# A fixed emitted order for attention pieces and MLP groups in a fused attention and MLP kernel

## The chip, the core and the metric

The kernel runs on one core of a Trainium2 chip. The time is device microseconds (us) of that core, as a median of several executions. The profile's span runs from the first to the last instruction and is a few us shorter. PE is the TensorE matmul engine, DVE is VectorE, ACT is ScalarE, POOL is GpSimd and SP is SyncE.

## The reference

Eight batches of eight heads, 576 tokens and 64 columns of q, k and v go through linear attention. Its output, 4608 tokens of 512 columns, goes through a two-layer MLP with squared ReLU.

```python
q_p = phi(q, cos_w, sin_w)     # relu(x)*cos beside relu(x)*sin: 128 features
k_p = phi(k, cos_w, sin_w)
kv  = einsum('bhsf,bhsd->bhfd', k_p, v);  z = sum(k_p, axis=2)
num = einsum('bhsf,bhfd->bhsd', q_p, kv)
den = einsum('bhsf,bhf->bhs', q_p, z)[..., None] + 1e-06
x   = (num / den)              # rearranged to [4608, 512]
h   = x @ w_in                 # 512 -> 2048: "the first matmul"
out = relu(h)**2 @ w_out       # 2048 -> 512: "the second matmul"
```

## The kernel before

A batch of attention has three sorts of work on PE. `kz` is 40 matmuls of 65 columns. Then each of the five slices of tokens takes eight transposes (`tps`), eight matmuls (`numh`) and four more transposes. Between them DVE copies a result out of PSUM or divides. The tail of each batch has 64 tokens, the other slices 128.

```python
def attention_batch(b):
    ...                                            # loads, K features, V cast on ACT, kz
    for j, rows in slices:
        ...                                        # qp: cosine half on DVE, sine half on ACT
        for h in range(H):                         # PE
            nc.tensor.transpose(tps[:, h, :rows], qp[:rows, h, :], ident[:rows, :rows])
        nc.vector.tensor_copy(out=qpT[:, :, :rows], in_=tps[:, :, :rows])     # DVE
        for half in range(2):
            ...                                    # numh matmuls on PE; den, rden, attn on DVE
        for blk in range(NB):                      # PE
            nc.tensor.transpose(tps2[:, blk, :rows], attn[...], ident[:rows, :rows])
        nc.vector.tensor_copy(out=xT_dest(b, j, rows), in_=tps2[:, 0:NB, :rows])

def mlp_chunk(c):                                  # 512 tokens: 64 + 64 matmuls of 512 columns
    for hb in range(HB): ...                       # hps (PE), relu (ACT), square (DVE)
    for tt in range(NTT): ...                      # yps (PE), copy (ACT), store (SP)

for b in range(B):
    attention_batch(b)
for c in range(NCH):
    mlp_chunk(c)
```

The source puts all attention first. The instructions don't run in that order: a scheduler orders each engine's instructions, and it moves MLP matmuls up among the attention.

## Time and profile before

| | |
|---|---|
| median of three executions | 393.36 us (392.95 to 394.4) |
| span of the profiled execution | 388.8 us |
| PE busy | 335.3 us, 86% |
| pure MLP at the end | 13.81 us per 64 matmuls, 216 ns each |
| all 1152 MLP matmuls at that rate | 248.6 us |

These are lines of the page for the kernel before: busy tenths in 40 slices of 9.7 us each, where 9 is 90% or more, then the granted PE clock in tenths.

```profile
PE   0014586999999797999999999999999999999995
PEclk9999999899899698999999999999999999999999
```

PE does almost nothing in the first three slices of the span and is mostly full from the eighth on. The last part of the chain of waits, in order of time (start us, length us, what), is MLP alone.

```profile
204.81 13.81 PE yps L298 x64
218.62 13.81 PE hps L283 x64
...
356.75 13.81 PE hps L283 x64
370.57 13.83 PE yps L298 x64
```

That leaves 388.8 - 248.6 = 140 us which are not MLP at full rate: the start, and what attention costs after its gaps are filled with MLP. The three largest waits of PE in this kernel (who waited for whom: us in total, times, longest) are these.

```profile
PE kz L203 <- ACT kp L175: 22.5, 1, 22.5
PE tps L268 <- DVE attn L260: 9.4, 10, 1.1
PE numh L244 <- DVE qpT L235: 5.7, 9, 1.1
```

The first is the start. The other two are rare: 10 and 9 times, where attention has 40 slices of tokens (eight batches of five). The rest was covered by MLP matmuls. The clock's behaviour can be read from PE's timeline before (start us, length us, line, operation, count).

```profile
66.55 0.28 PE L268 MATMUL tps<-ident,attn 128*128 128x128 bf16 x2 [1.04 <-DVE attn L260]
...
67.58 3.11 PE L283 MATMUL hps<-xT,w1sb 128*128 128x512 bf16 x7
...
70.79 1.46 PE L283 MATMUL hps<-xT,w1sb 128*128 128x512 bf16 x6
```

After a thin stretch (one in which PE has little to do) seven matmuls take 3.11 us, 427 ns from start to start; soon after, six of the same shape take 1.46 us. The rate had halved against the 216 ns of pure MLP, then came back.

### The profile page before, as it was taken

Reading aid. Unit: us, or ns where it says so; the run is one execution under the profiler, and the core shown is the slowest. Engines: PE = TensorE matmul, PEld = TensorE weight load, DVE = VectorE, ACT = ScalarE, POOL = GpSimd, SP = SyncE. Lnnn points to the kernel's source line nnn. Section 1 sums busy time; section 2 is a strip of 40 time slices with the busy share of each in tenths; the row PEclk is TensorE's granted clock in tenths of the full one; section 3 lists DMA queues with packets and bytes.
Section 4 is the critical chain, followed back from the end, with each engine's and each line's share of the span. In section 5 each row is a group of like instructions: output and inputs, shape, how many; then the busy total and the mean of one; then the engine's idle time right before and its main releaser. Section 6 shows DMA issues by size and latency. Waiting matters only on the chain.

```text
span 388.8 us, 5849 instructions
## 1 busy us (share of the span) xinstructions
PE 335.3 (86%) x2272; PEld 173.0 (44%) x2272; DVE 173.0 (44%) x553; ACT 185.3 (48%) x319; POOL 2.9 (1%) x10
## 2 busy tenths in 40 slices
PE   0014586999999797999999999999999999999995
PEld 0013444565555454655544444444444444444442
DVE  1002757879687888584870150240330420420410
ACT  1063718689565758323642461551551642633621
POOL 3000000000000000000000000000000000000000
PEclk9999999899899698999999999999999999999999
DMA  8999861958859424242001101202102103002013
GB/s 218 225 214 304 258 200 25 362 198 253 248 166 306 131 78 139 65 127 66 1 2 52 57 0 54 56 0 64 46 0 83 27 6 77 28 27 79 4 27 83
DMA packets 45755, 42.32 MB, mean 109 GB/s; under 512 B 13984, under 2 KB 40608, under 8 KB 45728
## 3 DMA queue, kind: packets, MB, share of 16 engines
q1 hardware_dynamic: 43136, 37.76, 32.7%
q0 software_dynamic: 2592, 4.19, 5.8%
q8 instruction: 18, 0.29, 0.3%
q14 instruction: 9, 0.07, 0.1%
HBM read 36.70 MB, written 9.44 MB: 119 GB/s over the span
## 4 chain that ended last, share of the span: by engine, by line
PE 79%; DVE 8%; DMA 6%; SPq 2%; issue 2%; ACT 1%; ACTq 0%
PE yps L298 32%; PE hps L283 31%; DMA Qb<-in_q_dram 6%; PE tps L231 5%; PE kz L203 4%; PE tps L268 3%; PE numh L244 3%; DVE qpT L235 2%; SPq L156 2%; DVE attn L260 1%; DVE kp L167 1%; DVE qp L215 1%; DVE xT L273 1%; DVE den L252 1%; ACT vext L181 1%
## 5 line engine op out<-in xcount | busy, mean ns | idle before, releaser
L283 PE MATMUL hps<-xT,w1sb 128*128 128x512 bf16 x576 | 138.2, 389 | 0.5 <-DVE xT L273 0.5
L298 PE MATMUL yps<-w2sb,gT 128*128 128x512 bf16 x576 | 132.7, 382 | 1.6 <-DVE gT L292 0.8
L292 DVE TENSOR_TENSOR gT<-rt 128x512 bf16<-128x512 bf16 x144 | 60.4, 420 | 129.3 <-ACT rt L291 128.3
L291 ACT ACTIVATE rt<-hps 128x512 bf16<-128x512 f32 x144 | 85.3, 596 | 46.9 <-PE hps L283 45.0
L298 PEld LDWEIGHTS <-gT 128*128 128x128 bf16 x576 | 55.2, 98 | 63.8 <-issue 1.8
L283 PEld LDWEIGHTS <-w1sb 128*128 128x128 bf16 x576 | 55.3, 100 | 61.9 <-issue 4.6
L306 ACT COPY ysb<-yps 128x512 f32<-128x512 f32 x36 | 21.0, 585 | 84.0 <-PE yps L298 83.8
L203 PE MATMUL kz<-vext,kp 128*128 128x65 bf16 (+1 forms) x320 | 26.4, 204 | 27.7 <-ACT kp L175 22.5
L223 ACT ACTIVATE qp<-Qb,sin_col 128x512 bf16<-128x512 f32 x32 | 22.9, 719 | 27.8 <-PE tps L231 13.3
L203 PEld LDWEIGHTS <-kp 128*128 128x128 bf16 (+1 forms) x320 | 18.5, 100 | 34.6 <-ACT kp L175 24.6
L231 PE MATMUL tps<-ident,qp 128*128 128x128 bf16 (+1 forms) x320 | 29.3, 236 | 4.1 <-ACT qp L223 4.1
L260 DVE TENSOR_TENSOR attn<-numh,rden 128x256 bf16<-128x256 f32 (+1 forms) x80 | 32.1, 414 | 0.2
L268 PE MATMUL tps<-ident,attn 128*128 128x128 bf16 (+1 forms) x160 | 23.2, 232 | 9.6 <-DVE attn L260 9.4
L235 DVE COPY qpT<-tps 128x1024 bf16<-128x1024 bf16 (+1 forms) x40 | 25.3, 634 | 11.8 <-PE tps L231 11.3
L181 ACT CAST vext<-Vb 128x512 bf16<-128x512 f32 x32 | 18.4, 611 | 18.6 <-DMA Vb<-in_v_dram 18.6
L231 PEld LDWEIGHTS <-qp 128*128 128x128 bf16 (+1 forms) x320 | 21.9, 109 | 5.8 <-ACT qp L223 4.2
L268 PEld LDWEIGHTS <-attn 128*128 128x128 bf16 (+1 forms) x160 | 12.5, 103 | 25.8 <-DVE attn L260 17.6
L244 PE MATMUL numh<-kvz,qpT 128*128 128x65 bf16 (+1 forms) x320 | 18.7, 204 | 5.7 <-DVE qpT L235 5.7
L244 PEld LDWEIGHTS <-qpT 128*128 128x128 bf16 (+1 forms) x320 | 14.8, 107 | 19.0 <-DVE qpT L235 15.3
L175 ACT ACTIVATE kp<-Kb,sin_col 128x512 bf16<-128x512 f32 x32 | 21.7, 713 | 0.5 <-DMA Kb<-in_k_dram 0.5
L273 DVE COPY xT<-tps 128x512 bf16<-128x512 bf16 (+1 forms) x40 | 15.8, 394 | 11.5 <-PE tps L268 11.3
L215 DVE TENSOR_SCALAR qp<-Qb,cos_col 128x512 bf16<-128x512 f32 x32 | 15.1, 476 | 10.4 <-DMA Qb<-in_q_dram 10.4
(24 smaller groups left out, 74.0 us busy)
## 6 DMA issues: line engine op xcount, KB each, us to landing
Kb<-in_k_dram SPq DMA_DIRECT2D x8, 1024.0 KB, 7.8
Vb<-in_v_dram SPq DMA_DIRECT2D x8, 1024.0 KB, 10.8
Qb<-in_q_dram SPq DMA_DIRECT2D x8, 1024.0 KB, 5.5
out_dram<-ysb SPq DMA_DIRECT2D x40, 128.0 KB, 2.3
out_dram<-ysb SPq DMA_DIRECT2D x16, 256.0 KB, 2.4
w1sb<-in_moe_w_in_dram POOLq DMA_DIRECT2D x1, 2048.0 KB, 17.9
w2sb<-in_moe_w_out_dram POOLq DMA_DIRECT2D x1, 2048.0 KB, 32.2
Kt<-in_k_dram SPq DMA_DIRECT2D x8, 128.0 KB, 8.9
```

Source lines behind the costliest of these rows:

```text
L181: nc.scalar.copy(out=vext[:rows, j, :, 0:D], in_=vsrc)
L203: nc.tensor.matmul(out=kz[:, hh, :], lhsT=kp[:rows, j, h, :], rhs=vext[:rows, j, h, :], start=(ji == 0), stop=(ji == len(slices) - 1),)
L223: nc.scalar.activation(out=qp[:rows, :, D:F], in_=qsrc, func=ACTF.Relu, scale=sin_col[:rows, j : j + 1],)
L231: nc.tensor.transpose(tps[:, h, :rows], qp[:rows, h, :], ident[:rows, :rows])
L235: nc.vector.tensor_copy(out=qpT[:, :, :rows], in_=tps[:, :, :rows])
L244: nc.tensor.matmul(out=numh[:rows, hh, :], lhsT=qpT[:, h, :rows], rhs=kvz[:, h, :], start=True, stop=True,)
L260: nc.vector.tensor_tensor(out=attn[:rows, half * HH : half * HH + HH, :], in0=numh[:rows, :, 0:D], in1=rden[:rows].unsqueeze(2).to_broadca ...
L268: nc.tensor.transpose(tps2[:, blk, :rows], attn[:rows, 2 * blk : 2 * blk + 2, :], ident[:rows, :rows],)
L283: nc.tensor.matmul(out=hps[:, :], lhsT=w1sb[:, kb, hb * P : (hb + 1) * P], rhs=xT[:, kb, t0 : t0 + CH], start=(kb == 0), stop=(kb == KB - 1),)
L291: nc.scalar.activation(out=rt[:, :], in_=hps[:, :], func=ACTF.Relu)
L292: nc.vector.tensor_tensor(out=gT[:, hb, :], in0=rt[:, :], in1=rt[:, :], op=ALU.mult)
L298: nc.tensor.matmul(out=yps[:, :], lhsT=gT[:, hb, tt * P : (tt + 1) * P], rhs=w2sb[:, hb, :], start=(hb == 0), stop=(hb == HB - 1),)
```

## The change

The change has three intents. The order of every engine is fixed as emitted. The attention of batches 2 to 7 is put in pieces between groups of MLP matmuls, and the first matmul runs ahead of the second, so that the second matmul never waits for the square. All transposes stay on PE. Evictions also become wider (1024 columns for the first matmul), the V cast moves from ACT to POOL, and weights and later batches load behind the first two batches. The core of the diff, with cuts:

```diff
+PE_TRANSPOSE_BATCHES = 8
 ...
+    def att_v(b, j):
+        nc.gpsimd.tensor_copy(out=vexts[b % 2][:rows, j, :, 0:D], in_=piece("v", b, j))
 ...
+    def att_q(b, j):
+        qp = att.tile([P, H, F], BF16, name="qp", tag="qp", bufs=3)
+        feats(qp, piece("q", b, j), j, rows)                  # DVE and ACT
 ...
+        if b < PE_TRANSPOSE_BATCHES:
+            tq = ps_h.tile([P, H, P], BF16, name="tq", tag="hps", bufs=2)
+            for h in range(H):
+                nc.tensor.transpose(tq[:, h, :rows], qp[:rows, h, :], ident[:rows, :rows])
+            nc.vector.tensor_copy(out=qpT[:, :, :rows], in_=tq[:, :, :rows])
 ...                                                       # else: transposes by DMA
+    def att_out(b, j):          # num on PE; den, rden, x on DVE; tx on PE; copies to xT on DVE
 ...
-    for b in range(B):
-        attention_batch(b)
-    for c in range(NCH):
-        mlp_chunk(c)
+    with tc.manual_schedule():
+        ...
+        for b in range(2):                                    # the opening: no MLP in it
+            ...
+            att_kv(b, 0)
+            att_kv(b, 1)
+            for j in range(NS):
+                att_q(b, j)
+                att_out(b, j)
+        ...
+        gemm1_with_k(0, B)
+        gemm1_with_k(1, B)
+        for r in range(NCH):                                  # a round; b = r + 2
+            ...
+            for tt in range(NTT):
+                gemm2(r, tt)                                  # 16 matmuls
+                if b < B:
+                    if tt == 0:
+                        att_kv(b, 0)
+                        att_kv(b, 1)
+                        for j in range(NS):
+                            att_q(b, j)
+                    elif tt == 1:
+                        att_out(b, 0)
+                        att_out(b, 1)
+                        att_out(b, 2)
+                    elif tt == 2:
+                        att_out(b, 3)
+                        att_out(b, 4)
+            if r + 2 < NCH:
+                gemm1_with_k(r + 2, b + 1)
```

## The prediction

> **What bounds it now.** PE. The page gives PE 335 of 388.8 us (86%). From 204.8 us on, the chain of waits is pure MLP, 64 matmuls per 13.81 us (216 ns each), so all 1152 MLP matmuls need 248.6 us. The other 140 us are: no real PE work until about 29 us (loads, V casts), then eight attention batches. Between 29 and 204.8 us, 320 MLP matmuls (69 us) ran as filler in the attention's gaps, so attention costs about 13 us a batch beyond the MLP, of which 8.8 us is PE work (timeline: kz 40 x 73 ns, numh 8 in 0.55-0.6, transposes 8 in 0.45 and 4 in 0.25).
>
> **What the change does.** Little work is removed (fewer, wider evictions; V casts go from ACT to POOL). The order becomes literal on every engine. PE takes no filler, so each PE-DVE-PE round trip inside a piece is PE idle time.
>
> *Opening.* Batches 0 and 1 run alone, with no MLP. Loads no longer share with the weights; loads without them show 340-386 GB/s, so V0 is in at about 9 us, POOL casts end at about 12 (estimate; the Trainium skill, GPSIMD Engine Reference, Engine selection, calls one-input work roughly line-rate; no trace here shows it yet), kz ends at 16. Each slice is then serial: 8 cold transposes 0.87, copy 0.69, numh 0.62, den 0.16, reciprocal 0.17, multiply about 0.68 (estimated from 256 columns at 0.415), transposes 0.43, copy 0.42, next features 0.48, plus hops: 4.95 us. Ten slices and the second kz: first MLP matmul at about 73 us.
>
> *Rounds with attention (6).* kz 2.8. Queries: kz end, ACT eviction 0.38, ACT sine feature 0.72 before the first transpose; then per slice transposes 0.46, DVE copy 0.69, DVE feature of the next slice 0.48 and hops, 1.73: section 8.7 with 2.3 us of PE work. Outputs: numh 0.55, den+reciprocal+multiply 1.0, transposes 0.25, hops: 1.96 per slice, 9.8 with 4 us of PE work. Sum 21.3 us a round, 12 of it PE idle.
>
> *Clock.* The Trainium skill (TensorE: Matmul & The Clock Gate, Part 1) states half clock after an idle window of about 3.4 us and recovery after as long a busy one. The trace before agrees: after the sparse 62-67 us, seven hps matmuls take 3.11 us (427 ns, not 216), then full speed. Each sparse section should make the following group of 16 MLP matmuls about 1.5 us longer and its own transposes slower: about 4.5 us a round.
>
> ACT in the first matmul's groups: eviction of 1024 about 1.02 plus sine feature 0.72 equals PE's 1.73 per pair: about 0.5 us a round.
>
> **Sum.** Opening 73; two first chunks 29; six rounds of 27.6+21.3+4.5+0.5 = 323; last rounds 55; tail 4; launch difference 4.6 (393.4 against 388.8): 489. I lean a little lower for overlap I miss: **482 us, 445 to 515**. Chances: faster 0.03, same 0.03, slower 0.94.
>
> **What would show it.** First hps matmul at 65-80 us. In rounds: tq waits for DVE qp and the copy, tx waits for the DVE multiply, each several tens of us of PE idle in the groups; PE busy share falls to about 65-75%; granted clock below 0.95; first matmul's groups nearly gapless; windows of pure MLP at the end still 13.81 us per 64.
>
> **What would make it wrong.** Opening much shorter than 73 (warm clock, quicker slices); clock staying full in rounds (27 us less); DVE and PE pieces overlapping more than the literal order allows; POOL casts or POOL-issued loads arriving late (longer).

## The result, and the profile after

The changed kernel took 499.62 us (498.64 to 500.66, 4 runs) against 393.17 us for the kernel before. The ratio is 1.2708 (95% interval 1.2678 to 1.2738). Here and below, a ratio is the mean time of one kernel's runs over that of the kernel before in the same rounds, so it is not quite the ratio of the medians quoted. Executions over 1.5% slower than the fastest of the same kernel are left out of the means.

The same lines of the page, now for the changed kernel in slices of 12.4 us:

```profile
PE   0545439995689666985689567986689567999996
PEclk9999999995799768995899677995899778999999
```

PE is idle in the first slice of the span, about half busy in the next five, full for three, and then shows six rounds in which its busy share and its clock fall and rise together. These are its main waits for other engines.

```profile
PE tx L242 <- DVE x L225: 49.8, 40, 1.4
PE tq L197 <- DVE qp L145: 36.1, 30, 1.3
PE tq L197 <- ACT qp L153: 11.2, 10, 1.3
```

The counts are the point. There are 40 slices of tokens, and PE waited before `tx` 40 times and before `tq` 40 times. Before the change, the corresponding waits were 10 for `attn` and one for `qp`. The Trainium skill says that PE keeps matmuls in program order and only pulls weight loads ahead (TensorE: Matmul & The Clock Gate, Part 2). The trace agrees: in the rounds, ready MLP matmuls stand behind the 60 waits before `tq` and `tx` and don't overtake them.

One slice of the opening (start us, length us, engine, what) shows the serial chain.

```profile
23.64 1.01 PE L197 MATMUL tq<-ident,qp 128*128 128x128 bf16 x8 [1.13 <-DVE qp L145]
24.69 0.69 DVE L198 COPY qpT<-tq 128x1024 bf16<-128x1024 bf16 x1 [1.20 <-PE tq L197]
25.44 0.62 PE L210 MATMUL num<-kvz,qpT 128*128 128x65 bf16 x8 [0.79 <-DVE qpT L198]
26.54 0.69 DVE L225 TENSOR_TENSOR x<-num,rden 128x512 bf16<-128x512 f32 x1
27.28 0.61 PE L242 MATMUL tx<-ident,x 128*128 128x128 bf16 x4 [1.22 <-DVE x L225]
28.90 1.01 PE L197 MATMUL tq<-ident,qp 128*128 128x128 bf16 x8 [1.00 <-DVE qp L145]
```

A bracket is the idle time of the line's own engine just before it, and what ended it. From one `tq` to the next is 5.26 us, in which PE works for 2.2. The first MLP matmul starts at 74.84 us. One round, from PE's timeline:

```profile
160.99 3.62 PE L298 MATMUL yps<-w2sb,gT 128*128 128x512 bf16 x16
164.45 1.50 PE L176 MATMUL kz<-vext,kp 128*128 128x65 bf16 x20
166.41 1.50 PE L176 MATMUL kz<-vext,kp 128*128 128x65 bf16 x20 [0.46 <-ACT kvz L183]
168.99 1.03 PE L197 MATMUL tq<-ident,qp 128*128 128x128 bf16 x8 [1.09 <-ACT qp L153]
171.30 1.01 PE L197 MATMUL tq<-ident,qp 128*128 128x128 bf16 x8 [1.27 <-DVE qp L145]
...
178.64 5.59 PE L298 MATMUL yps<-w2sb,gT 128*128 128x512 bf16 x16
184.07 0.42 PE L210 MATMUL num<-kvz,qpT 128*128 128x65 bf16 x8
185.71 0.40 PE L242 MATMUL tx<-ident,x 128*128 128x128 bf16 x4 [1.22 <-DVE x L225]
...
190.02 5.04 PE L298 MATMUL yps<-w2sb,gT 128*128 128x512 bf16 x16
...
198.73 3.63 PE L298 MATMUL yps<-w2sb,gT 128*128 128x512 bf16 x16
202.20 13.98 PE L268 MATMUL hps<-xT,w1sb 128*128 128x512 bf16 x64
```

Taken by the starts, the four groups of `yps` took 3.46, 5.43, 4.88 and 3.47 us for the same 16 matmuls. The middle two follow thin stretches of 14.2 and 5.9 us, and were slow in all six rounds. The fourth also follows a thin stretch, of 3.8 us, but was slow in only one round of the six (5.15 us). The whole time after splits up at the starts of groups as follows.

| part | predicted us | measured us |
|---|---|---|
| to the first MLP matmul | 73 | 74.8 |
| two chunks of the first matmul | 29 | 30.3 |
| six rounds with attention | 323 | 332.8 (55.5 on average) |
| last rounds without attention | 55 | 55.3 |
| tail, and launch outside the span | 8.6 | 6.4 |

### The profile page after: what moved, and what is told of

It reads as the page before. It is cut to its first block, busy times and chain, and to the rows that moved or that the text cites. A ratio compares the mean times of both kernels' runs of the same rounds, so it can differ in the third digit from the quotient of the medians.

```text
span 497.9 us, 5606 instructions
## 1 busy us (share of the span) xinstructions
PE 371.0 (75%) x2272; PEld 190.5 (38%) x2272; DVE 164.4 (33%) x359; ACT 152.6 (31%) x207; POOL 57.9 (12%) x92
## 5 line engine op out<-in xcount | busy, mean ns | idle before, releaser
L298 PE MATMUL yps<-w2sb,gT 128*128 128x512 bf16 x576 | 152.1, 428 | 0.0
L276 ACT ACTIVATE rt<-hps 128x1024 bf16<-128x1024 f32 x72 | 73.7, 1023 | 59.6 <-PE hps L268 57.2
L277 DVE TENSOR_TENSOR gT<-rt 128x1024 bf16<-128x1024 bf16 x72 | 49.9, 693 | 114.4 <-ACT rt L276 114.4
L197 PE MATMUL tq<-ident,qp 128*128 128x128 bf16 (+1 forms) x320 | 36.1, 286 | 47.3 <-DVE qp L145 36.1
L242 PE MATMUL tx<-ident,x 128*128 128x128 bf16 (+1 forms) x160 | 17.7, 244 | 49.8 <-DVE x L225 49.8
L198 DVE COPY qpT<-tq 128x1024 bf16<-128x1024 bf16 (+1 forms) x40 | 25.5, 638 | 84.5 <-PE tq L197 84.5
L197 PEld LDWEIGHTS <-qp 128*128 128x128 bf16 (+1 forms) x320 | 27.5, 131 | 55.6 <-ACT qp L153 27.5
L176 PE MATMUL kz<-vext,kp 128*128 128x65 bf16 (+1 forms) x320 | 27.5, 206 | 17.8 <-POOL vext L165 12.1
L176 PEld LDWEIGHTS <-kp 128*128 128x128 bf16 (+1 forms) x320 | 19.9, 101 | 26.6 <-issue 10.9
L225 DVE TENSOR_TENSOR x<-num,rden 128x512 bf16<-128x512 f32 (+1 forms) x40 | 27.6, 690 | 1.4
L210 PE MATMUL num<-kvz,qpT 128*128 128x65 bf16 (+1 forms) x320 | 19.0, 207 | 7.3 <-DVE qpT L198 7.3
L153 ACT ACTIVATE kp<-k,sin_col 128x512 bf16<-128x512 f32 x32 | 21.9, 711 | 3.5 <-DMA k<-in_k_dram 3.5
L153 ACT ACTIVATE qp<-q,sin_col 128x512 bf16<-128x512 f32 x32 | 20.8, 714 | 0.2 <-ACT qp L153 0.2
L210 PEld LDWEIGHTS <-qpT 128*128 128x128 bf16 (+1 forms) x320 | 15.6, 109 | 13.2 <-DVE qpT L198 9.8
```

The source lines that it names most:

```text
L153: nc.scalar.activation(out=dst[:rows, :, D:F], in_=src, func=ACTF.Relu, scale=sin_col[:rows, j : j + 1])
L176: nc.tensor.matmul(out=kz[:, half, hh * E1 : (hh + 1) * E1], lhsT=kp[:rows, j, h, :], rhs=vx[:rows, j, h, :], start=(j == 0), stop=(j == J),)
L197: nc.tensor.transpose(tq[:, h, :rows], qp[:rows, h, :], ident[:rows, :rows])
L198: nc.vector.tensor_copy(out=qpT[:, :, :rows], in_=tq[:, :, :rows])
L210: nc.tensor.matmul(out=num[:rows, h // HH, e0 : e0 + E1], lhsT=qpT[:, h, :rows], rhs=kvz[:, h, :], start=True, stop=True,)
L225: nc.vector.tensor_tensor(out=x[:rows], in0=n4[:, :, :, 0:D], in1=rden[:rows].unsqueeze(3).to_broadcast([rows, 2, HH, D]), op=ALU.mult,)
```

## The experiments

All kernels below gave a correct result. First the four that take the cost apart: the clock, one link of the chain, where the pieces stand, and the order as such.

### warm: fill PE's gaps with useless matmuls

```diff
+            dummies(4 if j == 0 else 5)   # 128x512 into the PSUM tile of the next yps group,
+                                          # whose first matmul overwrites it
             for h in range(H):
                 nc.tensor.transpose(tq[:, h, :rows], qp[:rows, h, :], ident[:rows, :rows])
 ...
+            dummies(5)                    # and before each slice's tx, in the rounds
```

> The changed kernel with four or five useless 128x512 matmuls in each of the ten gaps of a round where PE waits for DVE or ACT (before each group of tq or tx); they write into the PSUM tile of the next group of MLP matmuls, which overwrites it. They fit into the gaps (5 x 0.216 = 1.08 us of 1.2 to 1.3). Theory 1 (gaps plus a clock that falls because of them): the gaps keep their length, the clock stays full, so only the clock's share goes: about 6.5 us in each of six rounds, 499.6 falls to about 460; yps groups all take 3.45 us. Rival (the slow yps groups are slow for another reason, such as PSUM or SBUF traffic, not the clock): no gain, 500 or a little more.

It took 466.95 us (466.7 to 469.5), ratio 1.1885, with a mean granted clock of 0.991 against 0.893. Lines of PE's timeline, inside a query section and after it (`L318` is the real second matmul, `L195` the useless ones):

```profile
117.72 0.61 PE L214 MATMUL tq<-ident,qp 128*128 128x128 bf16 x8 [0.19 <-DVE qp L145]
118.16 1.24 PE L195 MATMUL yps<-w1sb 128*128 128x512 bf16 x5
119.59 0.61 PE L214 MATMUL tq<-ident,qp 128*128 128x128 bf16 x8 [0.19 <-DVE qp L145]
...
121.78 3.63 PE L318 MATMUL yps<-w2sb,gT 128*128 128x512 bf16 x16
```

PE did more work and the kernel got 32.7 us faster, or 5.4 us per round (6.5 were expected). The same 16 `yps` matmuls now take 3.47 us from start to start, and `tq` repeats every 1.87 us instead of 2.28. So the slow `yps` groups were slow through the clock, and the rival falls. What remains of the loss is the chain itself, which the useless matmuls only cover up.

### feat_ahead: take one link out of the chain

```diff
-                        for j in range(NS):
-                            att_q(b, j)
+                        att_qf(b, 0)                    # features only
+                        for j in range(NS):
+                            if j + 1 < NS:
+                                att_qf(b, j + 1)
+                            att_qt(b, j)                # transposes and copy only
```

> The changed kernel with one move: in the rounds, the query features of slice j+1 are emitted before the transposes of slice j, so that DVE makes them while PE transposes. Theory 1 (each gap is the literal DVE queue's serial chain: copy 0.69, then feature 0.48): four gaps of 1.27 us shrink to about 0.2 to 0.7 each, 2 to 4 us a round, 475 to 488 us. Rival (the gaps are fixed hand-over latency between the engines, or the clock): under 1 us a round, 494 to 500.

It took 472.99 us (471.12 to 474.61), ratio 1.2022. That is 26.6 us less, or 4.4 us per round, just beyond the expected 2 to 4. PE's timeline in the first round, then PE's waits in all rounds (105 to 425 us), for the changed kernel (`L197`) and for this run (`L206`):

```profile
113.56 1.87 PE L206 MATMUL tq<-ident,qp 128*128 128x128 bf16 x16 [1.09 <-ACT qp L153]
115.85 1.67 PE L206 MATMUL tq<-ident,qp 128*128 128x128 bf16 x16 [0.42 <-DVE qp L145]
118.52 0.39 PE L206 MATMUL tq<-ident,qp 64*128 64x64 bf16 x8 [1.00 <-DVE qp L145]
```

```profile
PE tq L197 <- DVE qp L145: 27.9, 22, 1.3
PE tq L206 <- DVE qp L145: 3.5, 7, 1.0
```

The gaps of 1.27 us are partly gone and no longer stand before every slice. With those for ACT, which changed little (9.1 and 9.7 us), the waits before `tq` fell from 37.0 to 13.2 us: 24 of the 26.6 us. Moving a slice's features ahead in the queues of DVE and ACT did that, with no work removed. The slow clock was not cured. In the second round the four `yps` groups took 17.8 us together, against 17.2 in the changed kernel: the two in the middle became shorter (4.8 and 4.4 us), but the fourth was now slow too, at 5.15 us, and so in every round.

### spread: the same pieces, one at a time

```diff
-            for tt in range(NTT):
-                gemm2(r, tt)
-                ...                                     # five tq, three outputs, two outputs
+            for u in range(4 * NTT):
+                gemm2(r, u // 4, u % 4)                 # four matmuls, 0.86 us
+                for f, bb, j in gaps[u]:                # kz half | kz half | tq0 | tq1 | num0 |
+                    f(bb, j)                            # tq2 tx0 | num1 | tq3 tx1 | num2 | ...
```

> The changed kernel with the same operations, but in the six rounds each attention piece (kz half, one slice's tq, num or tx) stands alone behind four MLP matmuls (0.86 us) of the second matmul instead of five together behind sixteen; opening untouched. Theory 1 (PE idles because the pieces stand together, and the clock falls because of that): per round 12.9 us of idle and about 6.5 us of slow clock nearly vanish, a round falls from 55.8 to 37.5-39.5 us, total 390 to 405. Rival (transposes on PE and their PSUM share cost this much wherever they stand): over 470.

It took 393.02 us (392.76 to 393.21), ratio 0.9991: the whole loss of the change is gone, with the opening as slow as it was. PE's timeline in the first round, then PE's waits in the rounds after it (148 us to the end):

```profile
120.76 0.61 PE L206 MATMUL tq<-ident,qp 128*128 128x128 bf16 x8
121.28 0.40 PE L261 MATMUL tx<-ident,x 128*128 128x128 bf16 x4
121.52 1.03 PE L321 MATMUL yps<-w2sb,gT 128*128 128x512 bf16 x4
122.38 0.42 PE L221 MATMUL num<-kvz,qpT 128*128 128x65 bf16 x8
```

```profile
PE tx L261 <- DVE x L236: 3.0, 10, 0.4
```

The second round took 36.6 us from its first `yps` to the next round's (148.12 to 184.69), against 55.0 in the changed kernel. The transposes are the same number, on the same engine and in the same PSUM buffers. It is where the pieces stand that costs. That includes feat_ahead's move: spread, too, makes the query features of a slice some pieces before its `tq` (not shown in the cut), and this run doesn't say how the gain divides between the two.

### free_order: the new program, ordered by the scheduler

```diff
-    with tc.manual_schedule():
+    if True:
```

> The changed kernel's program without the fixed order: the scheduler orders each engine's instructions as it does for the kernel before. Theory 1 (the literal order is what costs): the scheduler fills the gaps with MLP matmuls, 360 to 420 us. Rival (the new program itself, with wide evictions, one PSUM buffer for kz and num, and transposes in the first matmul's PSUM buffers, costs it): over 460.

It took 380.13 us (379.44 to 380.34), ratio 0.966. So the new program as such is a little better than the kernel before; the fixed order made it 120 us slower. The scheduler did not repair the opening: its first MLP matmul starts at 68.9 us. In the rounds it put MLP matmuls between the pieces, much as spread does by hand:

```profile
114.63 0.42 PE L210 MATMUL num<-kvz,qpT 128*128 128x65 bf16 x8
115.11 1.46 PE L298 MATMUL yps<-w2sb,gT 128*128 128x512 bf16 x6
116.40 0.39 PE L242 MATMUL tx<-ident,x 128*128 128x128 bf16 x4
```

### before_literal: the old program, in its source order

```diff
-    for b in range(B):
-        attention_batch(b)
-    for c in range(NCH):
-        mlp_chunk(c)
+    with tc.manual_schedule():
+        ...                                             # the same two loops
```

> The kernel before, its operations and buffers unchanged, with the same fixed-order region around its loops: all eight batches of attention in the order of the source, then the nine MLP chunks. Theory 1 (before, the scheduler's filling of attention's gaps with MLP was what kept it at 393): each slice costs about 5 us cold as in the opening of the changed kernel, a batch 28 to 33 us, total 500 to 550 us. Rival (order matters little, the other parts of the change cost the time): under 420.

It took 540.69 us (540.45 to 541.01), ratio 1.3815 (95% interval 1.3734 to 1.3897; the record's automatic verdict is "unclear", for a reason it doesn't give, but the interval lies far above 1). A batch of attention alone takes 31.8 us from `tq` to the next batch's `tq` (67.84 to 99.64 us). Together with free_order this closes the square: old program 393 free and 541 literal, new program 380 free and 500 literal. The change's pieces between MLP groups were thus better than no mixing at all, but worse than the mixing that the scheduler already did.

### dma_t: take the transposes of six batches off PE

```diff
-PE_TRANSPOSE_BATCHES = 8
+PE_TRANSPOSE_BATCHES = 2
```

> The changed kernel with its own switch set to 2: batches 0 and 1 are transposed on PE as before, batches 2 to 7 by DMA, in the same fixed order. Theory 1 (in this order the cost is that PE waits in place): the waits before tq and tx in the rounds (12.4 us each round) and 3.5 us of PE work go, and most of the slow clock, if the transposing DMAs keep up: 370 to 410 us. Rival (a DMA round trip is longer than the DVE one, and PE waits for it in the same place): 470 or more.

It took 424.05 us (421.33 to 426.4), ratio 1.0834. This missed the expected range of 370 to 410. The waits before `tq` and `tx` in the rounds are gone, as expected, but the trace's waits of PE in the rounds show what came in their place:

```profile
PE num L210 <- DVE x L225: 34.8, 18, 3.3
PE num L210 <- DMA qpT<-qp: 8.8, 5, 6.5
```

The waits listed for the changed kernel in its rounds came to 74.6 us (`tx` and `tq`); these two come to 43.6. `num` has one PSUM buffer. With the `tx` transposes gone from between two `num` groups, the next group waits for DVE to empty it, and some waits reach 3.3 us. Behind several of them stands a transposing DMA. Before one of 2.98 us (`num` at 166.69), the features of the fourth and fifth slices stood ahead of the division in DVE's queue, and the first of them had waited 7.72 us for such a DMA to read its `qp` buffer, of which there are three; DVE waited so 12 times, 56.8 us in all. Before one of 2.21 us, DVE's multiply itself had waited 0.93 us for a DMA that was still to read its buffer. The DMAs took a median of 2.9 to 3.0 us from issue to landing. So more than half of the wait changed its place rather than vanishing, and the mean clock was still 0.959. "PE waits in place" held. The condition in the expectation, that the transposing DMAs keep up, did not, and a part of the rival (PE waits for the DMA in its place) was right, though not its 470 us. No run gave `num` or `qp` another buffer, so the shares of the two causes are not known.

### ahead and ahead2: mix everywhere

Ahead keeps the fixed order, but moves attention one batch further ahead. Batch 0 stands alone, batches 1 and 2 go between the units of the first two chunks, and batches 3 to 7 are spread over whole rounds. The first matmul evicts 512 columns at a time again, so that the transposes can have two PSUM banks of their own.

```diff
+        run(u1(0), att_gaps(1))           # a unit is 4 matmuls; one piece behind every unit
+        load_batch(3, nc.gpsimd)
+        run(u1(1), att_gaps(2))
+        for r in range(NCH):
+            if r + 4 < B:
+                load_batch(r + 4, nc.gpsimd)
+            run(u2(r) + (u1(r + 2) if r + 2 < NCH else []), att_gaps(r + 3))  # behind every 2nd
```

> The fixed order kept, but attention one batch further ahead and spread over everything: batch 0 alone with features emitted a slice ahead, batches 1 and 2 between the units of the first two chunks, batches 3 to 7 one piece behind every eight MLP matmuls of five rounds; the first matmul evicts 512 columns at a time, transposes have their own two PSUM banks. Theory 1 (every gap can be covered when a piece of MLP as long as the DVE round trip stands between two pieces, and the opening costs what MLP it lacks): batch 0 done at about 32, two chunks with a batch each 24 to 27 us, five rounds of about 37, 55 and 28 without attention, 353 to 365 us in all; faster than both kernels. Rival (an in-order plan can't do better than the scheduler's): 380 or more.

It took 362.91 us (361.36 to 364.38), ratio 0.9273 (0.923 to 0.9316), faster than both kernels. Several things changed at once here, so the gain over spread can't be divided among them. The largest wait left but the start was this:

```profile
PE tx L261 <- DVE x L236: 15.4, 18, 2.0
```

Ahead2 moves `tx` in the list of pieces, and with it the places where the next batch's K features and V casts are emitted:

```diff
-        [(nm, 0)], [(qt, 2), (tx, 0), (qf, 3)],
-        [(nm, 1)], [(qt, 3), (tx, 1), (qf, 4)],
+        [(nm, 0)], [(qt, 2), (qf, 3)], [(tx, 0), (nm, 1)], [(qt, 3), (qf, 4)],
 ...
```

> The run ahead with only the order of the pieces moved: between a slice's num and its tx stand two units of MLP and often the next slice's tq, instead of one unit (tx of slice j shares a gap with num of slice j+1). In ahead, PE still waited 15.4 us in 18 places for DVE's x before tx. Theory 1 (a piece waits exactly where less MLP stands between two pieces than the DVE round trip takes): those waits shrink to under 4 us, total 349 to 356. Rival (DVE is by now full in the first two chunks, so the wait only moves elsewhere): 359 to 365.

It took 351.87 us (351.37 to 352.86, 6 runs), ratio 0.8947 (0.8903 to 0.8991). The same wait is now:

```profile
PE tx L261 <- DVE x L236: 8.3, 9, 1.5
```

The time fell into the expected range, by 11.0 us; the wait shrank by 7.1, to 8.3 us rather than below 4. PE's busy time fell as well, from 323.9 to 319.4 us with the same work, so not all of the gain is this wait. Of the 8.3 us, 5.4 lie in batch 0 (before 32 us), which has no MLP to stand between its pieces; from there on 2.9 us are left. In five windows of 37 us in the rounds (81 to 266 us) PE is busy for at least 36.6 us each.

### ahead_free: the scheduler orders ahead's program

```diff
-    with tc.manual_schedule():
+    if True:
```

> The run ahead with the fixed order taken away: the scheduler orders its instructions. Theory 1 (order is the cause, and a scheduler's order covers most but not all gaps): 355 to 380, no better than the fixed one. Rival (the scheduler always beats a fixed order): under 350.

It took 358.35 us (357.29 to 359.34), ratio 0.9107. The scheduler's order beat ahead's, where "no better than the fixed one" was expected (ahead ran in another batch, but the intervals of the two ratios, 0.923 to 0.9316 and 0.9056 to 0.9158, don't meet). It lost to ahead2's by 6.5 us (these two ran in the same rounds on one chip). A fixed order is as good as its pieces are placed.

## Why the prediction was right

- "PE takes no filler, so each PE-DVE-PE round trip inside a piece is PE idle time." Shown: 40 and 40 waits in the trace. In each round PE waited 12.9 us, where "12 of it PE idle" was predicted. Spread removes nearly all of the rounds' waits by where the pieces and their features stand, and the time goes from 499.6 to 393.0; free_order removes most of them by leaving the order to the scheduler.
- "First MLP matmul at about 73 us." It was 74.84. A slice took 5.26 us, not 4.95: eight cold transposes took 1.01, not 0.87, and four took 0.61, not 0.43. What made up for it are the tail slices, which the prediction counted as full ones: batch 0's took 3.6 us, from its `tq` at 39.40 to the next batch's K features at 42.98. The ten slices took 49.1 us against 49.5, two errors that cancel, which is luck. The 1.8 us that remain come from the start: the first `tq` began at 18.24 us, and the prediction's slices at 16.
- The round's outputs section, "9.8": 5.95 + 3.83 = 9.78 us. The waits of 1.22 to 1.30 us before `tx` were as costed.
- The round's kz and queries, 2.8 + 8.7 = 11.5: mis-sized, 14.2 us (164.45 to 178.64). Two terms failed. The prediction took a slice's query step as 1.73 us, and it was 2.28. Of the 0.55 us, 0.41 go with the low clock, which began with this section (the step is 1.87 in warm); the rest fits eight transposes that the profile ends 0.61 us after their start even at full clock, and not 0.46. It also took the two halves of `kz` as back to back, but the second waits 0.46 us for ACT's copy of the first. Both halves lie in one PSUM tile here; the kernel before gives each its own, and its list of waits has none of PE for that copy.
- "Clock: about 4.5 us a round": warm gives 5.4. The mechanism held, the count did not: the prediction's 4.5 is three groups of 1.5 us, but the third thin stretch slowed the group after it in only one round of six, and the other two groups lost more, 2.0 and 1.4 us in the round shown. There the `yps` groups lost 3.4 us in all (17.2 instead of 13.8); the rest of the 5.4 is about what the slow transposes above cost. That 4.5 came so near is in part luck. "Granted clock below 0.95" held, at 0.893.
- "About 0.5 us a round" for ACT in the first matmul's groups was not there: 64 matmuls took 13.81 us, with evictions of 1.02 us as estimated.
- The sum, 489, was nearer than the centre of 482 that it was lowered to "for overlap I miss". No such overlap shows in the table above; the 7 us taken off were the largest single part of the miss of 17.6 us besides the rounds, which took 332.8 us instead of 323.
- "PE busy share falls to about 65-75%": 75%.

What is left open: how far the opening itself can fall. Batch 0 alone still takes 32 us in ahead2, bound by its load, the V casts and the chain of DVE. No run tried to split that batch.

## What to carry to other kernels

When an order is fixed, don't count the work of a piece but its round trips: between two dependent pieces on PE there has to stand at least as much independent PE work as the other engine's answer takes, and an instruction for the next slice belongs in the answering engine's queue before the wait, not after it. A scheduler may already be filling such gaps, so compare a fixed order with the same program ordered freely before believing in it. Here thin stretches cost PE twice, once as idle time and once as a slow clock: in the dense group after the two longer ones (14.2 and 5.9 us) in every round, after the short one (3.8 us) in one round of six, and in all six of feat_ahead.

## What the Trainium skill lacked or had wrong

- TensorE: Matmul & The Clock Gate, HAM oscillation, gives as the rule "no PE-idle gaps >~3.4µs". That is not enough: in the round shown, PE had waited only 0.46 and 1.09 us since a dense group, and the next eight transposes already took 1.03 us instead of 0.61. Filling the gaps with matmuls mostly kept the clock up (the `yps` groups took 3.47 us instead of up to 6.21). The page itself says in its next section, on a second failure mode, that frequent short idles make the clock swing, but gives no measure of how much is too much; the runs here didn't settle it either.
- The same page warns in Part 1 that the recorded clock events can be unreliable, but not that a slow clock can be recorded as full. Here the record says 1.00 for the whole opening of 74.8 us, in which eight transposes take 1.01 us, and 0.999 for before_literal, with the same 1.01 us. The six runs of ahead2 lie within 0.5% of each other in time, with recorded clocks from 0.968 to 0.996. The durations show the slow clock, the record doesn't always; why was not looked into.
- The page's half rate and recovery agree with this: 3.11 us for seven matmuls after a thin stretch (427 ns from start to start), 216 ns for one in the dense end.
- GPSIMD Engine Reference, Engine selection, calls one-input work roughly line-rate but has no time for a cast. Here a cast of 128x512 from f32 to bf16 took a mean of 615 ns on POOL (690 in ahead2; spans on POOL are rough), against 611 ns on ACT before.
- DMA: Bandwidth & Descriptors, DMA Transpose, states constraints but no time to landing for a small transpose from SBUF to SBUF. Here those of `qpT` in dma_t (128x1024 bf16, in one slice of five 64x1024) took a median of 2.9 us from issue to landing, up to 9.0.
